# A decode step on one core: all eight sets in PE's loop, wide copies, and the first rows of wo loaded in strided pieces

## The chip, the cores and the metric

The kernel runs on one core of one Trainium2 chip. A core has a matrix engine (PE, whose weight loads are listed as PEld), a vector engine (DVE), a scalar engine (ACT), GpSimd (POOL), a sync engine (SP), and 16 DMA engines that move data between HBM and SBUF. The engines run their own instruction streams and meet at semaphores. DMA requests are issued here from SP and, a few, from ACT; each of the two has its own queue, and within a queue requests are served in order.

The metric is the time of one execution in device microseconds (us), as the median of several runs.

## The reference

One decode step for four batch rows `x` (4 x 512). It computes `g * a + (1 - g) * b`, all inputs bf16:

- `g = sigmoid(sum(x * gate_w))`, one number per row.
- `a`: attention with 32 query heads and 8 KV heads of width 128. `q = x @ wq` (512 x 4096). Each group of four query heads attends to the last 4096 positions of its KV head: scores `q . k / sqrt(128)`, softmax, weighted sum of `v`. The 4096 results per row are multiplied by `wo` (4096 x 512).
- `b`: `h = relu(x @ W_gate) * (x @ W_up)` (both 512 x 1792), then `h @ W_down` (1792 x 512).

There are 4 batch rows x 8 KV heads, so 32 pairs of a 4096 x 128 K block and a V block of the same size, 1 MB each. With the weights some 81 MB are read in all; the output is 4 KB.

## The kernel before, in words

The work is cut into eight **sets** (`NSET`): set s is batch row s // 2 with four KV heads (s % 2 says which half). The K of a set is one DMA of 4 MB into `Ksb[:, s % 2]`, its V one of 4 MB into `Vsb[:, s % 2]`; both are double-buffered. A partition of K holds 128 positions of one head.

Everything is written out by hand. A small class `Program` (line 38) records each engine's operations in order with the named events that each waits for, and emits them as semaphore waits. PE's list has a loop (`Fori`, line 134); all other engines' lists are straight.

Order of requests on SP: wq (line 568, before the block), K0, K1, V0, K2, V1, and so on (lines 231 to 234), then W_gate and W_up into K's buffer 0, V7, W_down into V's buffer 0, and wo in five pieces into `Wbig` (lines 243 to 249). Request K(s) waits until the last scores of set s - 2 are computed (`("SC", s-2, 3)`), V(s) until the last weighted sum of set s - 2 (`("PV", s-2, 3)`). `Wbig` holds wq first; so wo's requests wait for the event `Q`, the last product with wq.

Per set, in PE's order:

- `maximum(s-1)`, `exponent(s-1, k)`, `turn(s-1, k)`: the softmax of the set before. DVE reduces four maxima to a column (L398), PE spreads it over the partitions (L400), DVE takes the minimum (L403), ACT takes the exponential in two pieces of 1024 columns with their sums (L411), DVE transposes each piece in 32 x 32 blocks (L418).
- `kt(s, i)`, 16 **fills** per set: PE transposes four 128 x 128 blocks (two bf16 taken as one fp32) into one of four PSUM banks (L363), and ACT (11 of 16, `ACT_TAKES`) or DVE (the others) copies the bank back over K in SBUF (L368, L370).
- `scores(s, bank)`, four times: eight products of 512 columns on four 32-column strips of the array (L384); then one DVE pass adds the mask and takes the maximum (L392).
- `values(s-1, k)`: four times 16 products with V (L429), then ACT copies the sum (L435).
- `combine(s-2)`: 8 products that gather the heads (L443), the sums of the exponentials (L447), reciprocal and scaling on DVE (L450, L451).

Sets 0 and 1 are written straight on PE; sets 2 to 7 run as three turns of the loop, two sets each. After the loop: the softmax of set 7, `combine(6)`, `gateup` (L459), `values(7)`, `combine(7)`, then `product` (L530): 14 x 4 products with W_down and 32 x 4 with wo, each of 128 columns on one of four column strips, waiting for each piece of wo as it lands. ACT and DVE copy two strips each (L548, L550), and SP sends the output (L574).

## Time and profile before

| What | Value |
|---|---|
| Median of 3 runs | 196.29 us (196.19 to 196.31) |
| Profiled execution: span from first to last instruction | 194.9 us |
| Mean granted PE clock in it | 0.889 |
| Moved by DMA | 81.16 MB, mean 416 GB/s |
| PE, DVE, ACT, POOL busy | 139.4, 77.2, 76.1, 9.5 us |

The profile is of one execution of its own; no time but its span is recorded for it. The runs' median lies 1.4 us above that span, as the span begins with the first and ends with the last instruction on an engine.

How to read the rows that follow. The DMA line of the page cuts the span into 40 slices of 4.87 us; a digit is the mean busy share of the 16 DMA engines in tenths. The queue rows give packets, MB and the time that the packets took as a share of 16 engines' span. A row of the timeline reads: start, length, engine, line, operation, written tile <- read tiles, shapes, number of merged instructions, and in brackets how long the engine idled before and what ended that. A row of a group ends in busy time, mean length of one in ns, and the idle time before. A row of windows reads: stretch, its length, busy time of PE, PEld, DVE, ACT and POOL (number of instructions), the granted PE clock, the DMA share, GB/s. A row of a DMA issue ends in KB and the median us from the issue to the landing.

### The profile page before, as it was taken

Reading aid. Unit: us, or ns where it says so; the run is one execution under the profiler, and the core shown is the slowest. Engines: PE = TensorE matmul, PEld = TensorE weight load, DVE = VectorE, ACT = ScalarE, POOL = GpSimd, SP = SyncE. Lnnn points to the kernel's source line nnn. Section 1 sums busy time; section 2 is a strip of 40 time slices with the busy share of each in tenths; the row PEclk is TensorE's granted clock in tenths of the full one; section 3 lists DMA queues with packets and bytes.
Section 4 is the critical chain, followed back from the end, with each engine's and each line's share of the span. In section 5 each row is a group of like instructions: output and inputs, shape, how many; then the busy total and the mean of one; then the engine's idle time right before and its main releaser. Section 6 shows DMA issues by size and latency. Waiting matters only on the chain.

```text
span 194.9 us, 3931 instructions
## 1 busy us (share of the span) xinstructions
PE 139.4 (72%) x1728; PEld 103.6 (53%) x1728; DVE 77.2 (40%) x169; ACT 76.1 (39%) x140; POOL 9.5 (5%) x41
## 2 busy tenths in 40 slices
PE   0135399688789818996898189995995899643834
PEld 0112397366468517763685177854773777422633
DVE  0100045477268302762583026623952456280101
ACT  2005136494285404462854043445641545240001
POOL 8700000000000000000000000000000000000000
PEclk9999999999999995899999855799999579995855
DMA  6999999999999999999999999999999999998993
GB/s 216 444 437 430 430 444 434 430 430 430 440 430 417 437 427 430 437 437 427 430 430 444 430 437 430 430 430 430 430 430 430 430 386 427 479 430 381 429 397 102
DMA packets 3884, 81.16 MB, mean 416 GB/s; under 512 B 409, under 2 KB 930, under 8 KB 1058
## 3 DMA queue, kind: packets, MB, share of 16 engines
q1 hardware_dynamic: 3864, 81.01, 97.3%
q8 instruction: 8, 0.13, 0.3%
q14 instruction: 2, 0.02, 0.0%
q10 hardware_dynamic: 10, 0.01, 0.0%
HBM read 81.01 MB, written 0.00 MB: 416 GB/s over the span
## 4 chain that ended last, share of the span: by engine, by line
DMA 55%; PE 36%; ACT 4%; DVE 3%; issue 1%; SPq 1%; DVEq 0%
DMA Ksb<-in_A_k_cache_dram 43%; PE bank L363 23%; DMA Wbig<-in_A_wo_dram 11%; PE bank L384 6%; ACT Ksb L368 3%; PE bank L429 2%; PE bank L443 2%; DVE Ksb L370 1%; PE bank L530 1%; ACT L411 1%; ACT sc L411 1%; DVE pT L418 1%; PE bank L447 0%; DVE sc L392 0%; PE bank L400 0%
## 5 line engine op out<-in xcount | busy, mean ns | idle before, releaser
L363 PE MATMUL bank<-identw,Ksb 128*128 128x128 f32 x512 | 77.0, 307 | 20.8 <-DMA Ksb<-in_A_k_cache_dram 14.9
L363 PEld LDWEIGHTS bank<-identw,Ksb 128*128 128x128 f32 x512 | 65.3, 158 | 31.6 <-DMA Ksb<-in_A_k_cache_dram 15.8
L368 ACT COPY Ksb<-bank 128x512 f32<-128x512 f32 x88 | 48.7, 589 | 73.0 <-PE bank L363 73.0
L370 DVE COPY Ksb<-bank 128x512 f32<-128x512 f32 x40 | 27.3, 684 | 40.6 <-PE bank L363 40.6
L392 DVE CUSTOM_DVE_ANT_0 sc<-bank,mask 128x512 bf16<-128x512 f32 x32 | 21.8, 682 | 28.8 <-PE bank L384 28.8
L429 PE MATMUL bank<-Vsb,pT 128*32 128x256 bf16 x512 | 20.9, 291 | 6.1 <-DMA Vsb<-in_A_v_cache_dram 6.1
L384 PE MATMUL bank<-Ksb,qS 128*32 128x512 bf16 x256 | 21.0, 405 | 1.8 <-ACT Ksb L368 0.9
L418 DVE STREAM_TRANSPOSE pT<-sc 128x1024 bf16<-128x1024 bf16 x16 | 19.7, 1236 | 2.1 <-ACT sc L411 2.0
L429 PEld LDWEIGHTS bank<-Vsb,pT 128*32 128x32 bf16 x512 | 13.3, 101 | 12.6 <-issue 8.8
L411 ACT ACTIVATE sc<-sc,negmax 128x1024 bf16<-128x1024 bf16 x16 | 18.4, 1151 | 1.9 <-DVE negmax L403 1.8
L443 PEld LDWEIGHTS bank<-osb,Wsel 128*64 128x64 f32 x128 | 9.4, 157 | 4.8 <-issue 3.7
L443 PE MATMUL bank<-osb,Wsel 128*64 128x32 f32 x128 | 10.3, 239 | 0.5 <-ACT osb L435 0.5
L435 ACT COPY osb<-bank 128x256 f32<-128x256 f32 x8 | 3.0, 373 | 17.6 <-PE bank L429 17.6
L400 PE MATMUL bank<-identw,mcol 128*128 128x128 f32 x16 | 3.8, 320 | 7.8 <-DVE mcol L398 4.7
L384 PEld LDWEIGHTS bank<-Ksb,qS 128*32 128x32 bf16 x256 | 4.1, 95 | 9.0 <-ACT Ksb L368 5.7
L400 PEld LDWEIGHTS bank<-identw,mcol 128*128 128x128 f32 x16 | 2.4, 187 | 10.2 <-DVE mcol L398 8.4
L343 POOL COPY qS<-qW 128x64 bf16<-128x64 bf16 x8 | 1.8, 238 | 120.5 <-PE bank L384 110.8
L530 PE MATMUL bank<-Wbig,oq 128*4 128x128 bf16 x128 | 4.2, 307 | 3.8 <-DMA Wbig<-in_A_wo_dram 3.8
L296 PE MATMUL bank<-identw,xw 5*128 5x5 f32 x4 | 0.6, 263 | 8.6 <-DVE xw L290 8.6
L450 DVE RECIPROCAL recip<-bank 64x1 f32<-64x1 f32 x8 | 1.3, 159 | 11.4 <-PE bank L447 11.4
L530 PEld LDWEIGHTS bank<-Wbig,oq 128*4 128x4 bf16 x128 | 3.1, 118 | 4.8 <-DMA Wbig<-in_A_wo_dram 4.7
L314 PE MATMUL bank<-Wbig,xT 128*32 128x512 bf16 x32 | 3.6, 631 | 2.7 <-DMA Wbig<-in_A_wq_dram 2.7
(55 smaller groups left out, 45.4 us busy)
## 6 DMA issues: line engine op xcount, KB each, us to landing
Ksb<-in_A_k_cache_dram SPq DMA_DIRECT2D x8, 4096.0 KB, 21.8
Vsb<-in_A_v_cache_dram SPq DMA_DIRECT2D x8, 4096.0 KB, 30.9
Wbig<-in_A_wq_dram SPq DMA_DIRECT2D x1, 4096.0 KB, 12.2
Wbig<-in_A_wo_dram SPq DMA_DIRECT2D x1, 2048.0 KB, 19.5
Ksb<-in_B_W_gate_dram SPq DMA_DIRECT2D x1, 1792.0 KB, 17.1
Ksb<-in_B_W_up_dram SPq DMA_DIRECT2D x1, 1792.0 KB, 21.0
Vsb<-in_B_W_down_dram SPq DMA_DIRECT2D x1, 1792.0 KB, 15.0
Wbig<-in_A_wo_dram SPq DMA_DIRECT2D x1, 1280.0 KB, 22.1
```

What stands on the lines that cost most here:

```text
L314: P.op("pe", lambda e, half=half, t=t, g=g, col=col: e.matmul(SCB[half][32 * g:32 * g + 32, 0:512], xT[:, t, :], Wq3[:, t, col:col + 512], ...
L363: P.op("pe", lambda e, bk=bk, cc=cc, c=c, s=s: e.transpose(bk[:, cc * 128:(cc + 1) * 128], Kw[:, s % 2, c * 128:(c + 1) * 128], identw[:, :]),
L368: P.op("act", lambda e: e.copy(dst, bk[:, :]), ("KTC", s, i), [("KT", s, i)], sem="va")
L370: P.op("dve", lambda e: e.tensor_copy(dst, bk[:, :]), ("KTC", s, i), [("KT", s, i)], sem="vd")
L384: P.op("pe", lambda e, a=a, o=o: e.matmul(bk[32 * a:32 * a + 32, 0:512], qS[:, s % 2, o, :], k4[:, 16 * bank:16 * bank + 16, 32 * a:32 * a ...
L392: P.op("dve", lambda e: e.tensor_tensor_reduce(sc[:, s % 2, bank * 512:(bank + 1) * 512], bk[:, :], mask[:, :], 1.0, LOWEST, ALU.add, ALU.max,
L400: P.op("pe", lambda e: e.matmul(TR[NTR - 1][:, 0:128], mcol[:, par:par + 1].to_broadcast([128, 128]), identw[:, :], start=True, stop=True) ...
L411: P.op("act", lambda e: e.activation(sc[:, par, k * PW:(k + 1) * PW], sc[:, par, k * PW:(k + 1) * PW], ACTF.Exp, bias=negmax[:, par:par + ...
L418: P.op("dve", lambda e: e.transpose(pT[:, par, k * PW:(k + 1) * PW], sc[:, par, k * PW:(k + 1) * PW]), ("PTT", s, k), [("EXP", s, k), ("PV ...
L429: P.op("pe", lambda e, c=c, g=g, blk=blk: e.matmul(OB[32 * g:32 * g + 32, 0:256], pT[:, par, 32 * blk:32 * blk + 32], Vsb[:, par, 256 * bl ...
L443: P.op("pe", lambda e, k=k, lo=lo: e.matmul(FB[r, 384:416], Wsel[:, lo:lo + 64], osb[:, par, 32 * k:32 * k + 32], start=(k == 0), stop=(k ...
L530: P.op("pe", lambda e: e.matmul(AB[32 * cb:32 * cb + 4, 0:128], stat, mov[:, 128 * cb:128 * cb + 128], start=start, stop=stop, tile_positi ...
```

## The change

- *PE's loop.* All eight sets run in the loop, as four turns of two. Set -1 is a dummy: its `maximum` and its 64 `values` products run in the first turn on whatever lies there (pT's buffer 1 is zeroed by POOL, mx's too), and its result is not copied.
- *Wide operations.* A fill is eight transposes into two PSUM banks and one copy of 1024 columns; 8 fills per set, two buffers (`NTR`), 5 copies on ACT and 3 on DVE. Scores come in two pairs of banks: 16 products, one DVE pass of 1024 columns; the second pass starts its maximum from the first one's, so the separate reduction is gone. Exponential and DVE transpose take a set's 2048 columns at once. `values` runs its 64 products in one go after the last scores.
- *combine.* It is taken out of the sets. `osb` and `rowsum` keep all sets; after the loop `combine(0)` treats sets 0, 2, 4, 6 and, after the last `values`, `combine(1)` treats sets 1, 3, 5, 7, with 128-column products.
- *wq* is loaded into V's buffer 1 instead of `Wbig`, so V1's request now waits for the dummy `values(-1)`, and wo's requests wait for nothing.
- *wo.* The first three rows of each partition (3,072 bytes) are no longer in SP's pieces. ACT issues them after `gateup`'s ReLU, as twelve transfers: transfer a takes the partitions a, a + 12, a + 24, and so on, 11 in eight of them, 10 in four.
- *Products at the end.* Two strips of 256 columns instead of four of 128; one copy each on DVE and ACT.
- *Borders.* ACT, DVE and PE begin with an instruction that places the following one at a border of 128 (ACT, DVE) or 256 (PE) instructions.

```diff
-NTR = 4
-NSC = 2
-NPIECE = 2
-NBANK = 4
-NFILL = 16
-WO_CUTS = (0, 16, 26, 30)
-ACT_TAKES = (0, 1, 4, 6, 8, 9, 11, 12, 13, 14, 15)
-LOOP_FIRST = 2
-LOOP_TURNS = 3
+NTR = 2
+NPAIR = 2
+NFILL = 8
+WO_EARLY = 3
+WO_CUTS = (3, 16, 26, 30)
+ACT_TAKES = (1, 3, 4, 6, 7)
...
-        Wq3 = Wbig[:, :].rearrange("p (t w) -> p t w", t=4)
+        Wq3 = Vsb[:, 1, :].rearrange("p (t w) -> p t w", t=4)
...
         def load_v(s):
             P.dma("sp", lambda e: e.dma_start(Vsb[:, s % 2, :], heads(A_v_cache, s)), ("V", s),
-                  [("PV", s - 2, 3)] if s >= 2 else [], sem=loop_sem("V", s))
+                  [("PV", s - 2)] if s >= 1 else [], sem=loop_sem("V", s))
...
+        P.op("act", lambda e: e.addr_align(128, offset=0, max_nops=0))
+        P.op("dve", lambda e: e.addr_align(128, offset=0, max_nops=0))
+        P.op("pe", lambda e: e.addr_align(256, offset=0, max_nops=0))
...
-            P.dma("sp", lambda e, lo=lo, hi=hi: e.dma_start(Wbig[:, lo:hi], wo_src[:, lo:hi]), ("WO", k), [("Q",)])
+            P.dma("sp", lambda e, lo=lo, hi=hi: e.dma_start(Wbig[:, lo:hi], wo_src[:, lo:hi]), ("WO", k))
...
+            bk = TRT[:, 1024 * (f % NTR):1024 * (f % NTR) + 1024]
+            for cc in range(8):
+                c = 8 * i + cc
+                w = [("K", s), ("IDENTW",), fills[f - NTR] if f >= NTR else ("QR", 1, f)] if cc == 0 else []
...
+            P.op("dve", lambda e: e.tensor_tensor_reduce(
+                sc[:, s % 2, pair * 1024:(pair + 1) * 1024], SCT[:, :], mask[:, :], 1.0,
+                mx[:, s % 2, 0:1] if pair else LOWEST, ALU.add, ALU.max,
+                mx[:, s % 2, pair:pair + 1]), ("SCC", s, pair), w, sem="vd" if pair else "dve")
...
+            P.op("pe", lambda e: e.matmul(FB[:, 384:512], mx[:, par, 1:2].to_broadcast([128, 128]), identw[:, :],
+                                          start=True, stop=True),
+                 ("MT", s), [("SCC", s, 1)] if s >= 0 else [("XTC",)])
...
+        def values(s):
+            par = s % 2
+            for blk in range(64):
+                g = blk % 4
+                w = [("PTT", s), ("V", s), ("OSB", s - 1)] if blk == 0 else []
+                P.op("pe", lambda e, g=g, blk=blk: e.matmul(
+                    OB[32 * g:32 * g + 32, 0:256], pT[:, par, 32 * blk:32 * blk + 32],
+                    Vsb[:, par, 256 * blk:256 * blk + 256],
+                    start=(blk < 4), stop=(blk >= 60), tile_position=(0, 32 * g)),
+                    ("PV", s) if blk == 63 else None, w)
...
+        def combine(half):
...
+                P.op("pe", lambda e, k=k, lo=lo: e.matmul(CB[r, 0:128], Wsel[:, lo:lo + 64], ov[:, half, :, 32 * k:32 * k + 32],
+                                                          start=(k == 0), stop=(k == 7)), None,
+                     [("OSB", last), ("WSUM",)] + fills[-NTR:])
...
+        for s in range(NSET):
+            if s % 2 == 0:
+                P.turn_edge()
             maximum(s - 1)
+            exponent(s - 1)
+            for i in range(5):
+                kt(s, i)
+                if i == 2:
+                    turn(s - 1)
             scores(s, 0)
+            for i in range(5, NFILL):
+                kt(s, i)
             scores(s, 1)
+            values(s - 1)
         P.turn_edge()
         maximum(NSET - 1)
+        exponent(NSET - 1)
+        turn(NSET - 1)
+        combine(0)
         gateup()
+        early = 0
+        for n, (a, rows) in enumerate([(a, 11) for a in range(8)] + [(a, 10) for a in range(8, 12)]):
+            part = slice(a, a + 12 * (rows - 1) + 1, 12)
+            P.dma("act", lambda e, part=part: e.dma_start(Wbig[part, 0:512 * WO_EARLY], wo_src[part, 0:512 * WO_EARLY]),
+                  ("WOE", n), [], sem="wos")
+            early += 16
+        P.events[("WOE",)] = ("wos", early, None, 0)
+        values(NSET - 1)
+        combine(1)
...
+        def product(stat, mov, u, start, stop, name, waits):
+            P.op("pe", lambda e: e.matmul(AB[32 * u:32 * u + 4, 0:256], stat, mov[:, 256 * u:256 * u + 256],
+                                          start=start, stop=stop, tile_position=(0, 32 * u)), name, waits)
...
+        for i in range(WO_EARLY):
+            for u in range(2):
+                product(oq3[:, :, i], Wo3[:, i, :], u, False, False, None, [("WOE",), ("OQ", 0), ("OQ", 1)])
...
+        P.op("dve", lambda e: e.tensor_copy(outr[:, 0:256], AB[0:4, 0:256]), ("FIN", 0), [("ACC", 0)], sem="fin")
+        P.op("act", lambda e: e.copy(outr[:, 256:512], AB[32:36, 0:256]), ("FIN", 1), [("ACC", 1)], sem="fin")
...
-        nc.sync.dma_start(Wbig[:, :], A_wq.rearrange("(p t) w -> p (t w)", p=128)).then_inc(sems["wq"], 16)
+        nc.sync.dma_start(Vsb[:, 1, :], A_wq.rearrange("(p t) w -> p (t w)", p=128)).then_inc(sems["V1"], 16)
```

More of the change, by code (lines that the diff above doesn't have):

```diff
@@ L307, in bass_gated_mix__sliding_block_cached__glu_gated_reglu__decode_kernel @@
         P.op("act", lambda e: e.activation(gsb[:, 4:8], FB[:, 32:36], ACTF.Sigmoid, scale=-1.0), ("G",), sem="va")
-        for half in range(2):
-            for t in range(4):
+        for t in range(4):
+            for half in range(2):
                 for g in range(4):
@@ L389, in scores @@
-            w = [("SC", s, bank), ("MASK",)]
-            if s >= 2 and bank == 0:
-                w += [("PTT", s - 2, NPIECE - 1), ("MCOL", s - 2)]
+                for hb in range(2):
+                    for a in range(4):
+                        w = []
+                        if first:
+                            w = [("KTC", s, 4 * pair + u) for u in range(4)] + [("QS", s)]
+                            w.append(("SCC", s, 0) if pair else ("SCC", s - 1, 1) if s >= 1 else ("QR", 1, 1))
+                        first = False
+                        bank = 2 * pair + hb
+                        P.op("pe", lambda e, a=a, o=o, hb=hb, bank=bank: e.matmul(
+                            SCT[32 * a:32 * a + 32, 512 * hb:512 * hb + 512], qS[:, s % 2, o, :],
+                            k4[:, 16 * bank:16 * bank + 16, 32 * a:32 * a + 32, o], start=(o == 0), stop=(o == 1),
+                            tile_position=(0, 32 * a)),
+                            ("SC", s, pair) if (a == 3 and o == 1 and hb == 1) else None, w)
@@ L516, in bass_gated_mix__sliding_block_cached__glu_gated_reglu__decode_kernel @@
         P.turn_edge()
         maximum(NSET - 1)
-        for k in range(NPIECE):
-            exponent(NSET - 1, k)
-            turn(NSET - 1, k)
-        combine(NSET - 2)
+        exponent(NSET - 1)
+        turn(NSET - 1)
+        combine(0)
         gateup()
-        for k in range(4):
-            values(NSET - 1, k)
-        combine(NSET - 1)
-        AB = SCB[0]
+        early = 0
[4 more added lines that the diff above has]
+            early += 16
```

258 lines of the change are left out of this document (95 added, 163 removed).

## The prediction

> **What bounds the kernel now.** I read the page first: the span, the engines' shares, the DMA slices and the queues (packets, MB, share of 16 engines).
>
> ```profile
> span 194.9 us, 3931 instructions
> PE 139.4 (72%) x1728; PEld 103.6 (53%) x1728; DVE 77.2 (40%) x169; ACT 76.1 (39%) x140; POOL 9.5 (5%) x41
> DMA  6999999999999999999999999999999999998993
> q1 hardware_dynamic: 3864, 81.01, 97.3%
> q8 instruction: 8, 0.13, 0.3%
> q14 instruction: 2, 0.02, 0.0%
> q10 hardware_dynamic: 10, 0.01, 0.0%
> ```
>
> The 16 DMA engines are busy 97.3% of the span, while PE idles over a quarter of it. Moving 81 MB is the bound; what can be won lies where the DMA slices are not 9: the first slice (same requests, same order, after the change too) and the last few. So I cut the end into half microseconds (columns: length, then busy time of PE, PEld, DVE, ACT, POOL, then PE clock, DMA share, GB/s), and then read the timeline there (start, length, engine, line).
>
> ```profile
> 190.00:190.50 0.50, 0.00 (x0) 0.00 (x0) 0.00 (x0) 0.00 (x0) 0.00 (x0) 0.50 0.92 316
> 190.50:191.00 0.50, 0.09 (x8) 0.10 (x12) 0.00 (x0) 0.00 (x0) 0.00 (x0) 0.50 0.63 246
> 191.00:191.50 0.50, 0.50 (x24) 0.50 (x24) 0.00 (x0) 0.00 (x0) 0.00 (x0) 0.50 0.57 200
> 191.50:192.00 0.50, 0.50 (x26) 0.36 (x16) 0.00 (x0) 0.00 (x0) 0.00 (x0) 0.50 0.56 166
> 192.00:192.50 0.50, 0.50 (x24) 0.34 (x18) 0.00 (x0) 0.00 (x0) 0.00 (x0) 0.50 0.28 71
> ```
>
> ```profile
> 172.37 0.52 ACT L464 ACTIVATE hrelu<-bank 128x448 f32<-128x448 f32 x1
> 178.67 3.61 PE L429 MATMUL bank<-Vsb,pT 128*32 128x256 bf16 x64 [6.06 <-DMA Vsb<-in_A_v_cache_dram]
> 182.74 1.12 PE L443 MATMUL bank<-osb,Wsel 128*64 128x32 f32 x16 [0.47 <-ACT osb L435]
> 184.00 1.20 PE L530 MATMUL bank<-Vsb,hT 128*4 128x128 bf16 x56
> 187.77 1.88 PE L530 MATMUL bank<-Wbig,oq 128*4 128x128 bf16 x64 [2.57 <-DMA Wbig<-in_A_wo_dram]
> 190.91 2.30 PE L530 MATMUL bank<-Wbig,oq 128*4 128x128 bf16 x64 [1.25 <-DMA Wbig<-in_A_wo_dram]
> 192.82 0.10 PEld L530 LDWEIGHTS bank<-Wbig,oq 128*4 128x4 bf16 x4 [0.17 <-DMA Wbig<-in_A_wo_dram]
> 192.98 0.54 ACT L550 CAST outr<-bank 4x128 bf16<-4x128 f32 x2 [10.29 <-PE bank L530]
> 192.98 0.60 DVE L548 CAST outr<-bank 4x128 bf16<-4x128 f32 x2 [8.35 <-PE bank L530]
> 193.61 0.35 SPq L574 DMA_DIRECT2D out_dram<-outr  x1
> ```
>
> From 190.5 to 192.0 the share stands near 0.56, which is 9 engines of 16: seven have finished, nine run on. Every load gives each engine the same bytes, so something delayed nine. The page names it: ten instruction packets. The eight of q8 take 0.3% of 16 x 194.9, 9.4 us or 1.17 us each, and each sits on one engine. In half microseconds, 0.63 + 0.57 + 0.56 + 0.28 is 1.02 us of all engines; spread evenly it would end at 191.5 and not 192.5. PE waits for the last piece of wo until 192.82, so this unevenness is on the path, and so are the last copies.
>
> **The change part by part.**
>
> *Strided first rows of wo.* Three of the 32 rows of wo in each partition (128 pieces of 3,072 bytes) leave the SP queue for twelve ACT transfers of 11 or 10 rows. The queue q10 above carried a four-row and a one-row transfer in ten packets: five rows and five completions, so a short transfer uses as many engines as rows. If each begins at the same engine, ten engines take 12 rows, one takes 8 and five take none. 430 GB/s over 16 is 26.9 GB/s per engine: an even share is 24.6 KB or 0.91 us; 12 rows are 1.37 us. So five engines end 0.91 us earlier, ten 0.46 us later. If the five are the delayed ones, they end at 192.5 - 0.91 = 191.6, the others near 190.9 + 0.46 = 191.4: the last landing moves by -0.91. If they aren't, it moves by up to +0.46. I take -0.91: it is nearest to the 1.02 that an even end gives.
>
> [...]
>
> Twelve issues stand on ACT between the ReLU (172.37 + 0.52) and the last copy to osb, which needs the products that end at 182.28.
>
> ```profile
> 0.80 0.56 ACTq L229 DMA_DIRECT2D xsb<-in_A_x_dram  x1
> 1.40 0.23 ACTq L230 DMA_DIRECT2D xsb<-in_gate_w_dram  x1
> ```
>
> At 0.23 to 0.56 each they end at 175.7 to 179.6: covered; without cover up to 6.7 us. Without [Q], SP's wo requests only queue behind Wd's, as before.
>
> *All sets in PE's loop; borders.* Counted over the two programs, 956 PE products as written become 585, so the eight q8 packets should become about five, and the two of q14 go if ACT's and DVE's shorter programs fit their block. Five packets of 1.17 us over 16 engines are 0.4 us; zero if the remaining ones meet badly. I take -0.1. The jump to a border may cost PE, ACT or DVE a fetch at the start, but PE's first product waits until 8.57 for x, and set 0 until 22.72 for K. A loop fetched anew each turn would show in the middle; it doesn't, with two back edges inside:
>
> ```profile
> 8.57 0.64 PE L296 MATMUL bank<-identw,xw 5*128 5x5 f32 x4 [8.57 <-DVE xw L290]
> ```
>
> ```profile
> q1 hardware_dynamic: 1514, 37.83, 100.0%
> ```
>
> The second is the only queue row of 92 to 180 us.
>
> *Wide operations, and where they could let the DMA run dry.* These set when K and V buffers come free. Prices: twice the 512-wide rows, as upper bounds. The rows are groups (busy, mean ns), the timeline, and DMA issues (KB, us to landing: K2's alone, all K, wq).
>
> ```profile
> L368 ACT COPY Ksb<-bank 128x512 f32<-128x512 f32 x88 | 48.7, 589 | 73.0 <-PE bank L363 73.0
> L370 DVE COPY Ksb<-bank 128x512 f32<-128x512 f32 x40 | 27.3, 684 | 40.6 <-PE bank L363 40.6
> L392 DVE CUSTOM_DVE_ANT_0 sc<-bank,mask 128x512 bf16<-128x512 f32 x32 | 21.8, 682 | 28.8 <-PE bank L384 28.8
> ```
>
> ```profile
> 22.72 6.57 PE L363 MATMUL bank<-identw,Ksb 128*128 128x128 f32 x32 [4.50 <-DMA Ksb<-in_A_k_cache_dram]
> 29.77 1.97 PE L363 MATMUL bank<-identw,Ksb 128*128 128x128 f32 x16
> 163.75 0.62 PE L429 MATMUL bank<-Vsb,pT 128*32 128x256 bf16 x16
> ```
>
> ```profile
> Ksb<-in_A_k_cache_dram SPq DMA_DIRECT2D x1, 4096.0 KB, 17.5
> Ksb<-in_A_k_cache_dram SPq DMA_DIRECT2D x8, 4096.0 KB, 21.8
> Wbig<-in_A_wq_dram SPq DMA_DIRECT2D x1, 4096.0 KB, 12.2
> ```
>
> Eight transposes take 0.98 at full clock (1.97/2), a copy 1.2 to 1.4. With two buffers I follow the order: fills 0 to 4 end 5.8 us after K landed, first scores 7.0 (16 products, twice 0.62), fill 7 waits for DVE's copy behind its transpose and its masked pass and ends at 11.0, last scores 13.5, values 16.0 (four times 0.62). A set lasts 19.4 us by DMA. A K request lands after 21.8 us, its own 4.19 MB taking 9.7 and the start 12.2 - 9.7 = 2.5; so 9.6 us of delay are covered. Set 0 is tightest: K2's request (the 17.5 row, issued 35.68) has 5.3 us of cover, so until 41.0. Starting cold at 0.205 per transpose, I get the last score at 37.6. Covered by 3.4. The 64 dummy values of set 0 (2.5 us) delay V1's request to 40.1, behind the 9.7 us of K2; the two pool memsets and the wider mask end long before 35 us. The wait of each of these is PE's, and behind it stand only its own set's products. Cost nothing; uncovered, each us late is a us. Nothing here can gain, since the queue row above has the engines at 100.0%.
>
> *The end.* combine for all sets of a half comes after the last values: 16 products of 128 columns, 1.97 (as the transposes) and not 1.12. A product row now is two products of 256 columns on two column strips, not four of 128 on four: 256-column groups cost (0.62 - 0.27)/3 = 0.117 at full clock (0.27 being one product's length at the end of sixteen) and 3.61/16 = 0.226 at half. At full: 182.74 + 1.97 + 0.4 + 14 x 0.117 + 3 x 0.117 = 187.1, when wo's 13 rows have landed (187.77 - 0.91 = 186.9); they end at 188.6, the next ten (190.0) at 191.2, four at 191.7, and the last two, landing at 191.9, 0.39 later, against 0.16 before: +0.23. One 256-wide copy, 0.37 as the osb copy,
>
> ```profile
> L435 ACT COPY osb<-bank 128x256 f32<-128x256 f32 x8 | 3.0, 373 | 17.6 <-PE bank L429 17.6
> ```
>
> takes the place of two (0.60): -0.23.
>
> *Sum* against the profiled span: 194.93 - 0.91 - 0.10 + 0.23 - 0.23 = 193.92. The runs' median, 196.29, lies 1.36 above that span; I keep this: **195.3 us**.
>
> **The rivals.**
>
> *Half clock at the end (slower).* The clock rows, in its own windows:
>
> ```profile
> 117.40:120.80 3.40, 3.40 (x29) 2.23 (x27) 2.19 (x4) 1.65 (x3) 0.00 (x0) 0.50 1.03 443
> 178.80:182.20 3.40, 3.40 (x64) 2.57 (x57) 0.00 (x0) 0.00 (x0) 0.00 (x0) 0.50 1.01 429
> 182.20:185.60 3.40, 2.50 (x80) 2.04 (x76) 0.49 (x2) 0.37 (x1) 0.00 (x0) 1.00 0.98 411
> 185.60:189.10 3.50, 1.33 (x52) 1.33 (x56) 0.00 (x0) 0.00 (x0) 0.00 (x0) 0.51 0.98 410
> ```
>
> Before, the last products run at 0.50, which four strips can afford. With two strips at 0.226 the 13 rows end at 189.8, ten at 192.3, four at 193.2, the last four products near 194.0: 1.7 later than my 192.3, so **197.0**; half clock from the combine on would cost about 4. It decides if the clock is half when the ten rows land. For it: 185.6 on. Against: the longer streams are more work per window (1.5 us of wo's 13 rows beside 2.0 of Wd and the early rows, where a combine and 1.20 of short products lost it).
>
> [...] The trace agrees at 178.80 but not at 117.40, fully busy at 0.50 and followed by 0.50; so I leave this rival 17%.
>
> *Relief on the wrong engines (no change).* If fetches fall on the ten loaded engines, these end at 192.5 + 0.46, less what fewer fetches give (0.4): **196.3**. For: no row says which engines fetch. Against: nine were late before, so fewer must be now.
>
> *Set 0 late.* Cold clock through set 0: fills 8 x 1.7, scores 2 x 1.9, copies: the last score near 41.5, half a us dry: **195.8**; more if DVE's wide passes stall PE.
>
> **How the numbers follow.** Forecast 0.61, own range 194.5 to 195.7 (-1.02 and -0.4 in full below; half of the relief above); half clock 0.17; wrong engines 0.13; set 0 or a fetch stall 0.09 (half of it over 196.7). A measurement tells 0.2%, 0.4 us, from no change: faster 0.65 (the forecast and half of set 0), same 0.11 (wrong engines but for 0.02), slower 0.24 (half clock and the rest). The range, 194.5 to 197.0, reaches from the forecast's lower bound to half clock's price and leaves out the dearer half of that case and the worst stalls, under 0.2.
>
> **What would show it.** Right: q8 at five packets or fewer, q14 at none after the start; DMA share over 0.85 until it drops within half a us; the last wo landing near 191.9; middle windows at share 1.00. Wrong: share near 0.5 for over a us at the end (wrong engines), PE never waiting for wo at clock 0.50 (half clock), a slice under 9 near 41 us (set 0).

## The result, and the profile after

The changed kernel takes **199.45 us** (median, 199.33 to 199.51) against 196.25 for the kernel before on the same chip (196.19 to 196.31): a ratio of **1.0163** [1.0151, 1.0176]. It is slower by 3.2 us, where 195.3 was forecast and 194.5 to 197.0 given as the range. In the experiments, one execution each of three versions (without borders, twelve on SP's queue, four neighbouring) lay over 1.5% above that version's fastest and is left out of the times given below, so the four neighbouring stand at 198.34 where a later expectation has 198.46.

The page of the changed kernel (span; DMA share in 40 slices; queues with packets, MB, share of 16 engines):

```profile
span 198.2 us, 3511 instructions
...
PE 130.7 (66%) x1578; PEld 102.7 (52%) x1578; DVE 73.8 (37%) x95; ACT 66.4 (34%) x77; POOL 11.6 (6%) x43
...
DMA  6999999999999999999999999999999999999980
...
q1 hardware_dynamic: 3864, 80.61, 96.1%
q10 hardware_dynamic: 266, 0.40, 0.6%
q8 instruction: 5, 0.08, 0.2%
q14 instruction: 2, 0.02, 0.0%
```

The span grew from 194.9 to 198.2. No slice ran dry, and the engines do less work than before (PE 130.7 against 139.4). The same 81 MB took longer. Where, the windows show (length; busy time of PE, PEld, DVE, ACT, POOL; PE clock, DMA share, GB/s), first of the changed kernel, then of the kernel before:

```profile
60.00:170.00 110.00, 80.63 (x964) 65.01 (x963) 50.39 (x59) 43.40 (x47) 0.95 (x4) 0.91 1.00 430
...
176.50:181.00 4.50, 1.63 (x32) 1.42 (x36) 0.00 (x0) 0.00 (x0) 0.00 (x0) 0.56 0.98 372
181.00:187.00 6.00, 5.53 (x85) 4.52 (x75) 0.64 (x3) 0.37 (x1) 0.00 (x0) 0.76 1.00 363
187.00:191.50 4.50, 0.27 (x6) 0.00 (x0) 0.00 (x0) 0.00 (x0) 0.00 (x0) 0.91 0.99 355
191.50:195.00 3.50, 3.50 (x42) 2.37 (x44) 0.00 (x0) 0.00 (x0) 0.00 (x0) 0.63 0.46 166
```

```profile
176.50:181.00 4.50, 2.33 (x48) 2.03 (x51) 0.00 (x0) 0.00 (x0) 0.00 (x0) 0.50 0.97 412
181.00:187.00 6.00, 3.70 (x100) 2.73 (x92) 0.49 (x2) 0.37 (x1) 0.00 (x0) 0.78 1.00 419
187.00:191.50 4.50, 2.48 (x88) 2.19 (x92) 0.00 (x0) 0.00 (x0) 0.00 (x0) 0.50 0.88 347
191.50:195.00 3.50, 1.71 (x50) 0.95 (x40) 0.56 (x2) 0.52 (x2) 0.00 (x0) 0.50 0.12 35
```

From 176.5 on the engines are as busy as before (share 0.98 to 1.00) but move 372 and 363 GB/s in place of 412 and 419. A full share at a lower rate means that each packet takes longer (the records below: 0.61 us in place of 0.54). The timeline of the changed kernel (start, length, engine, line; in brackets the idle time before and what ended it) says what is in flight then:

```profile
24.56 6.47 PE L356 MATMUL TRT<-identw,Ksb 128*128 128x128 f32 x32 [3.37 <-DMA Ksb<-in_A_k_cache_dram]
...
39.10 0.53 SPq L218 DMA_DIRECT2D Ksb<-in_A_k_cache_dram  x1
...
172.43 9.39 ACTq L504 DMA_DIRECT2D Wbig<-in_A_wo_dram  x12
...
179.37 3.60 PE L425 MATMUL OB<-Vsb,pT 128*32 128x256 bf16 x64 [6.81 <-DMA Vsb<-in_A_v_cache_dram]
...
183.02 0.37 ACT L434 COPY osb<-OB 128x256 f32<-128x256 f32 x1 [10.06 <-PE OB L425]
...
191.50 4.91 PE L514 MATMUL SCT<-Wbig,oq 128*4 128x256 bf16 x64 [4.23 <-DMA Wbig<-in_A_wo_dram]
196.44 0.41 DVE L531 CAST outr<-SCT 4x256 bf16<-4x256 f32 x1 [10.05 <-PE SCT L514]
196.48 0.36 ACT L532 CAST outr<-SCT 4x256 bf16<-4x256 f32 x1 [13.09 <-PE SCT L514]
196.88 0.35 SPq L553 DMA_DIRECT2D out_dram<-outr  x1
```

The twelve strided transfers of wo are issued from 172.43 to 181.82. In the trace's packet records their rows run from 176.7 to 190.5, and exactly there a packet of SP's loads takes 1.15 times its usual length (median; 14,336 bytes: 0.61 us in place of 0.54). Only 5 of the 379 load packets in that stretch are within 3% of their usual length. The records do not name the engine. But in the kernel before, the first three loads of 4 MB start their packets of 32,768 bytes in 24 rounds of 16, eight rounds to a load (from 1.84 to 31.5 us), so the same bytes for every engine; if wo's pieces are dealt out alike, none of the 16 can have been spared. Before and after that stretch the factor is 1.00.

So the 3.3 us of span divide. The last packet of wo ends at 194.55 and not 192.37: **+2.2**. PE stands idle for the early rows until 191.50 and then has all 64 products of wo ahead of it, 4.91 us long, much of it at half clock (0.50 until 194.0); its last work ends at 196.44 and not 192.98, which is **+1.3** more than the landing. The copies to the output request take 0.44 in place of 0.63: **-0.2**.

### The profile page after: what moved, and what is told of

Same layout as the page of the kernel before. It is cut to its first block, busy times and chain, and to the rows that moved or that the text cites. A ratio compares the mean times of both kernels' runs of the same rounds, so it can differ in the third digit from the quotient of the medians.

```text
span 198.2 us, 3511 instructions
## 1 busy us (share of the span) xinstructions
PE 130.7 (66%) x1578; PEld 102.7 (52%) x1578; DVE 73.8 (37%) x95; ACT 66.4 (34%) x77; POOL 11.6 (6%) x43
## 4 chain that ended last, share of the span: by engine, by line
DMA 53%; PE 23%; DVE 13%; ACTq 4%; ACT 3%; issue 2%; PEld 1%; PEldq 0%; SPq 0%
DMA Ksb<-in_A_k_cache_dram 47%; PE TRT L356 14%; DVE Ksb L363 6%; DMA Wbig<-in_A_wo_dram 5%; ACTq L504 4%; DVE pT L417 3%; PE SCT L377 3%; ACT Ksb L361 3%; DVE sc L387 3%; PE SCT L514 3%; PE TRT L444 1%; PE OB L425 1%; PE TRT L461 1%; PEld OB L425 1%; PEldq L133 0%
## 5 line engine op out<-in xcount | busy, mean ns | idle before, releaser
L356 PE MATMUL TRT<-identw,Ksb 128*128 128x128 f32 x512 | 75.8, 309 | 24.2 <-DMA Ksb<-in_A_k_cache_dram 16.2
L356 PEld LDWEIGHTS TRT<-identw,Ksb 128*128 128x128 f32 x512 | 66.8, 160 | 34.4 <-DMA Ksb<-in_A_k_cache_dram 17.4
L361 ACT COPY Ksb<-TRT 128x1024 f32<-128x1024 f32 x40 | 40.5, 1012 | 57.9 <-PE TRT L356 57.8
L363 DVE COPY Ksb<-TRT 128x1024 f32<-128x1024 f32 x24 | 29.3, 1223 | 39.6 <-PE TRT L356 39.6
L425 PE MATMUL OB<-Vsb,pT 128*32 128x256 bf16 x576 | 18.9, 288 | 6.8 <-DMA Vsb<-in_A_v_cache_dram 6.8
L377 PE MATMUL SCT<-Ksb,qS 128*32 128x512 bf16 x256 | 16.9, 381 | 8.8 <-ACT Ksb L361 8.8
L425 PEld LDWEIGHTS OB<-Vsb,pT 128*32 128x32 bf16 x576 | 16.4, 101 | 9.7 <-issue 7.2
L387 DVE CUSTOM_DVE_ANT_0 sc<-SCT,mask,mx 128x1024 bf16<-128x1024 f32 x8 | 10.3, 1285 | 26.8 <-PE SCT L377 26.8
L407 ACT ACTIVATE sc<-sc,negmax 128x2048 bf16<-128x2048 bf16 x8 | 16.0, 2002 | 11.0 <-DVE negmax L399 11.0
L417 DVE STREAM_TRANSPOSE pT<-sc 128x2048 bf16<-128x2048 bf16 x8 | 18.4, 2302 | 2.2 <-ACT sc L407 2.2
```

The lines of the kernel that those rows point to most:

```text
L356: P.op("pe", lambda e, bk=bk, cc=cc, c=c: e.transpose(bk[:, cc * 128:(cc + 1) * 128], Kw[:, s % 2, c * 128:(c + 1) * 128], identw[:, :]), ...
L361: P.op("act", lambda e: e.copy(dst, bk), ("KTC", s, i), [("KT", s, i)], sem="va")
L363: P.op("dve", lambda e: e.tensor_copy(dst, bk), ("KTC", s, i), [("KT", s, i)], sem="vd")
L377: P.op("pe", lambda e, a=a, o=o, hb=hb, bank=bank: e.matmul(SCT[32 * a:32 * a + 32, 512 * hb:512 * hb + 512], qS[:, s % 2, o, :], k4[:, 16 ...
L387: P.op("dve", lambda e: e.tensor_tensor_reduce(sc[:, s % 2, pair * 1024:(pair + 1) * 1024], SCT[:, :], mask[:, :], 1.0, mx[:, s % 2, 0:1] ...
L407: P.op("act", lambda e: e.activation(sc[:, par, :], sc[:, par, :], ACTF.Exp, bias=negmax[:, par:par + 1], scale=SCALE, accum_out=rowsum[:, ...
```

## The experiments

The first question was whether the early rows are the loss at all; my theory after the result was that they are, through the slow packets. The rival was the change's other parts: the loop, the wide operations, the fetches at the start.

### Without the early rows

The twelve transfers go, `WO_CUTS` is `(0, 16, 26, 30)` again; loop, borders, wide operations and two strips stay.

```diff
-WO_CUTS = (3, 16, 26, 30)
+WO_CUTS = (0, 16, 26, 30)
-        early = 0
...
-        P.events[("WOE",)] = ("wos", early, None, 0)
```

> The changed kernel with wo's first three rows back in SP's first piece, nothing else undone. Theory 1 (the twelve early transfers cost it): DMA rate stays near 430 GB/s from 176 to 190 us, the last piece of wo lands near 192.8 and not 195.0, PE does not wait for early rows, time 195.8 to 196.6. Rival (the loop, the wide operations or the fetches at the start cost it, and the early transfers are only there beside it): time above 198.0, and the last landing stays late.

196.26 us (195.87 to 198.4), ratio 0.9999 [0.999, 1.0009]. In the median, the early rows are the whole loss. The landing did not come out as expected: the profiled execution is the longest of the eleven, 198.4, and its last packet of wo ends at 194.53, not near 192.8, although its packets keep their usual length (factor 1.00 from 176.7 to 190.5). The reason stands behind the table of packet records below.

### The borders, and borders and early rows together

```diff
-        P.op("act", lambda e: e.addr_align(128, offset=0, max_nops=0))
-        P.op("dve", lambda e: e.addr_align(128, offset=0, max_nops=0))
-        P.op("pe", lambda e: e.addr_align(256, offset=0, max_nops=0))
```

> The changed kernel without the three border alignments; the strided transfers stay. Theory 1 (the early transfers are the loss, and a code fetch costs one DMA engine 1 to 2 us wherever it falls, so moving the fetches to the start only moves that price): K0 lands about 1.8 us earlier, near 22.7, but fetches come back in the middle; 198.8 to 199.6. Rival (the start fetches are a price of their own that the missing middle ones do not give back): 197.4 to 198.4.

> The changed kernel with neither the early rows nor the three alignments: the loop over all sets, the wide operations, the shorter end and the two strips are left. Theory 1: within 0.3 of the kernel before, 195.9 to 196.5. Rival (the start fetches hide a gain of the loop and the wide operations): 194.4 to 195.4, and this version would beat both kernels.

Without the borders but with the early rows: median 198.91 us, but from 197.63 to 199.41, ratio 1.01 [1.007, 1.013]. The median lies where theory 1 put it; the scatter is too wide to weigh tenths. K0's first transpose is at 22.8 us again and not at 24.56: the 1.84 us of the start are the borders' price. With neither, 196.16 us, ratio 0.9994 [0.9985, 1.0003], beside 196.26 with the borders: in the median, the price at the start does not reach the end. In the median, the loop, the wide operations and the end of the changed kernel gain nothing and lose nothing that can be measured.

### One transfer, eight, twelve neighbouring

Why are the packets slow? One ACT transfer of 128 partitions; eight strided ones of 16 partitions, one row for every engine by their completions (q10 has 266 packets: the ten of before, 128 rows, and 128 completions, so 16 to a transfer); twelve of neighbouring partitions in place of strided ones.

```diff
-        for n, (a, rows) in enumerate([(a, 11) for a in range(8)] + [(a, 10) for a in range(8, 12)]):
-            part = slice(a, a + 12 * (rows - 1) + 1, 12)
# one
+        for n, part in enumerate([slice(0, 128)]):
# eight, stride 8
+        for n, a in enumerate(range(8)):
+            part = slice(a, a + 8 * 15 + 1, 8)
# twelve neighbouring
+        for n, (a, rows) in enumerate([(11 * a, 11) for a in range(8)] + [(88 + 10 * a, 10) for a in range(4)]):
+            part = slice(a, a + rows)
```

> The early rows as one ACT transfer of all 128 partitions in place of twelve. [...] If two active queues as such slow the packets: 14336-byte packets near 0.6 us for as long as it is in flight, and time above 198. If it is the assignment of partitions to engines (or the strided order in HBM) in the twelve: rate stays near 430 GB/s, time 195.8 to 196.8.

> [...] If it is the strided order in HBM, or two active queues, or many small transfers: rate near 360 GB/s while they are in flight, time above 198.

> The early rows as twelve ACT transfers of 11 or 10 neighbouring partitions: as many as before, the same engines by number of rows, but not strided. If it is the strided order in HBM: rate near 430 GB/s, time 196 to 197. If it is the assignment of partitions to engines, or two active queues: rate near 360 GB/s and time near 199.

One: 196.77 us, ratio 1.0048 [1.0017, 1.0079], packets at 1.01 times their length. Eight: 198.22, 1.01 [1.0083, 1.0117], packets at 1.24. Twelve neighbouring: 200.22, 1.0201 [1.0178, 1.0223], packets at 1.20. So a second queue as such does not slow the loads, and slow packets need neither a stride (the twelve neighbouring, at 200.22 even above the 199 expected) nor engines that get no rows (the eight). The assignment of partitions to engines seemed to be out too, because the eight were meant to keep the one of the large loads. But no row shows which engine writes which partition, so the price of the eight says nothing against the assignment, and the partitions come back below. At this point, what the dear ones had in common seemed to be that they are many and small.

### Many and small?

The twelve transfers put on SP's queue ahead of wo's first piece; four strided ACT transfers of 32 partitions; eight of 32 partitions and half the columns; four of 16 partitions and one of 64; five of 22 and one of 18.

```diff
# twelve on SP
+            P.dma("sp", lambda e, part=part: e.dma_start(Wbig[part, 0:512 * WO_EARLY], wo_src[part, 0:512 * WO_EARLY]),
# four, stride 4
+            part = slice(a, a + 4 * 31 + 1, 4)
# eight, stride 4, half the columns
+            part, cols = slice(n // 2, n // 2 + 4 * 31 + 1, 4), slice(768 * (n % 2), 768 * (n % 2) + 768)
# four of 16 and one of 64
+        for n, part in enumerate([slice(16 * a, 16 * a + 16) for a in range(4)] + [slice(64, 128)]):
# five of 22 and one of 18
+        for n, part in enumerate([slice(22 * a, min(22 * a + 22, 128)) for a in range(6)]):
```

> The same twelve strided transfers, put on SP's queue ahead of wo's first piece, so that they are alone in one queue with the loads and nothing is on ACT's queue. Theory 1a (many small transfers cost by themselves, in whatever queue): 197.0 to 199.0, with early rows' packets still slow. Theory 1b (they cost only beside a second queue's load, because each engine goes back and forth between two queues): 195.3 to 196.5, packets of 14336 B back at 0.54.

> The early rows in four ACT transfers of 32 partitions at stride 4, between the one transfer (196.77) and the eight (198.22). Theory 1 (the price grows with the number of transfers): 197.2 to 197.9, 14336 B packets at 0.56 to 0.62 while they are in flight. Rival (only transfers of 16 rows or fewer are dear): 196.3 to 196.9, packets at 0.54.

> Eight ACT transfers like the dear eight (198.22), but each of 32 partitions and half the columns (1536 B a row), so that every engine gets two rows of each transfer instead of one; the number of transfers and of their completions is the same. Theory 2 (what is dear is a transfer that gives an engine one single row): 196.1 to 196.8, 14336 B packets at 0.54. Rival (what is dear is the number of transfers and completions): 197.6 to 198.8, packets at 0.60 or more while they are in flight.

> Four ACT transfers of 16 partitions (one row an engine) for partitions 0 to 63, and one transfer for 64 to 127. Theory 2: half of the 64-of-128 single rows, so half of the loss of the eight: 196.9 to 197.6. Rival (five transfers are too few to hurt, as four were): 196.1 to 196.6.

> The early rows in five ACT transfers of 22 partitions and one of 18, two rows an engine, so that some engines are relieved of them as in the twelve, but without single rows. Theory 2: no slow packets; what is left is the relief: 195.3 to 196.4. Rival (leaving engines out is itself dear): 197.0 to 199.0.

On SP's queue: 199.81 us (198.82 to 200.02), above the 199.0 that theory 1a allowed. Here the early rows are alone in one queue with the loads, and while they run (180.3 to 185.5 in the packet records) the rate falls furthest:

```profile
176.50:180.50 4.00, 1.61 (x32) 1.41 (x36) 0.00 (x0) 0.00 (x0) 0.00 (x0) 0.50 0.95 402
180.50:185.50 5.00, 4.53 (x76) 3.85 (x69) 0.64 (x3) 0.37 (x1) 0.00 (x0) 0.88 1.06 263
185.50:190.00 4.50, 1.27 (x22) 0.58 (x16) 0.00 (x0) 0.00 (x0) 0.00 (x0) 1.00 0.96 389
```

Theory 1b, two queues, falls with that. Four at stride 4: 196.36, 1.0006 [0.9997, 1.0016], no slow packets. Eight at stride 4 with half the columns: packets at 1.01, which takes the number of transfers off the list. Its time, 198.14 (196.48 to 199.3; 1.0087 [1.0052, 1.0122]), is not explained by that: it missed theory 2's time while it bore out its packets. Its rows come in 256 smaller packets and land only at 189.6. Its last packet of wo ends at 193.94, 1.4 us later than with four transfers. In the profiled execution (198.89) about as much was lost long before the early rows, near 42 us, as shown behind the table of packet records.

Theory 2, single rows, fell with the other two: five transfers of 22 rows and one of 18, by my estimate two rows for each engine that takes part (four transfers of 32 rows had 202 - 10 - 128 = 64 completions, so 16 each), gave 199.04, 1.0147 [1.013, 1.0164], packets at 1.24. Four of 16 and one of 64 gave 198.93, 1.013 [1.0113, 1.0147], at 1.29, more than the rival's "too few to hurt" and more than the half that theory 2 allowed.

### Before the early rows are waited for

The products of the early rows moved behind those of wo's three pieces.

> The changed kernel, with the products of the early rows moved behind those of wo's three pieces: PE no longer stands still for the early rows. If the loss is PE's wait for them (4.23 us): 196.5 to 197.5. If it is the loads, of which the last lands 2.2 us later: the last landing stays near 195.0, the end moves by at most 1.2 us: 198.0 to 199.0.

The profiled execution took 198.47 us with a span of 197.2, 1.0 less than the changed kernel's, the last packet of wo at 194.53 as there. That fits: PE's wait is worth about 1, the loads the rest. But the median is 200.16 (198.47 to 201.01; 1.0217 [1.0191, 1.0242]), above both expected ranges, so the 1.3 of the split above is read from the trace and not confirmed by the runs.

### The place, the spread, and the change's other parts

The twelve transfers alone in the kernel before; four of 32 neighbouring partitions; two of 88 and 40 neighbouring ones; the twelve at the very start of ACT's program.

```diff
# four, neighbouring
+        for n, part in enumerate([slice(32 * a, 32 * a + 32) for a in range(4)]):
# 88 and 40
+        for n, part in enumerate([slice(0, 88), slice(88, 128)]):
```

> The kernel before with one part of the change alone: the twelve strided transfers on ACT's queue and the first three blocks of wo's products waiting for them. If the early rows are the whole loss, whatever loop and operations stand around them: 198.6 to 200.0, with 14336 B packets at 0.58 or more while they are in flight. If they only hurt together with the change's loop and wide operations: 195.5 to 196.6.

> Four ACT transfers of 32 neighbouring partitions instead of 32 at stride 4 (196.36). Theory 3 (what is dear is a transfer of fewer than 32 rows, wherever the rows lie): 196.1 to 196.8, packets at 0.54. Rival (what is dear is that the rows read at one time are neighbours, as in the contiguous twelve, the six and the half): 197.8 to 199.2, packets at 0.60 or more.

> Two ACT transfers, of 88 and of 40 neighbouring partitions, which leave engines out as the twelve do (88 rows as eight on each of eleven engines), but in large transfers. Theory 3 (few rows in a transfer are dear, not the uneven spread): packets at 0.54, 195.4 to 196.6. Rival (a spread over some of the engines alone is dear): packets at 0.60 or more, 197.8 to 199.5.

> The twelve strided transfers issued at the very start of ACT's program, beside the loads of wq and of the first K, instead of near the end. If the slow packets come with these transfers wherever they stand: K0 lands 2 to 4 us later than in the changed kernel and the end is 198.0 to 200.0. If they belong to the mix of loads at the end: 195.3 to 196.8, and this would be the way to have the early rows.

In the kernel before, the twelve alone cost 2.2 of the change's 3.2 us: 198.38 us, just under the 198.6 to 200.0 expected, 1.0134 [1.0092, 1.0176], packets at 1.15. At the start they slow K's packets instead, to 1.07 over 29 us. K0's first transpose comes at 26.00 and not 24.56, 1.4 us later where 2 to 4 were expected, and the end is late again: 198.59, 1.0126 [1.0108, 1.0144]. The 88 and 40: 198.93, 1.0153 [1.0092, 1.0213], at 1.28, so large transfers can be dear too. And four neighbouring: 198.34, 1.0112 [1.0092, 1.0132], at 1.24, where the same four at stride 4 cost nothing. Theory 3, few rows, is out as well. What is left is *which rows go where*.

### Which side of the transfer

Stride 4 in SBUF's partitions alone, and in the rows of wo alone.

```diff
+            part, rows = slice(a, a + 4 * 31 + 1, 4), slice(32 * a, 32 * a + 32)
# into partitions at stride 4, out of neighbouring rows
+            P.dma("act", lambda e, part=part, rows=rows: e.dma_start(Wbig[part, 0:512 * WO_EARLY], wo_src[rows, 0:512 * WO_EARLY]),
# into neighbouring partitions, out of rows at stride 4
+            P.dma("act", lambda e, part=part, rows=rows: e.dma_start(Wbig[rows, 0:512 * WO_EARLY], wo_src[part, 0:512 * WO_EARLY]),
```

> Four ACT transfers of 32 rows: into partitions at stride 4, as in the one that cost nothing (196.36), but out of neighbouring rows of wo, as in the one that cost 2 us (198.46). It puts wo's first three blocks in the wrong partitions, so these products are not the reference's. If what counts is which partitions an engine writes: packets at 0.54, 196.0 to 196.8. If what counts is which rows of wo are read at one time: packets at 0.60 or more, 198.0 to 199.2.

> The other way round: into 32 neighbouring partitions, out of rows of wo at stride 4 (again the wrong rows for the products). If what counts is which partitions an engine writes: packets at 0.60 or more, 198.0 to 199.2. If what counts is which rows of wo are read at one time: packets at 0.54, 196.0 to 196.8.

Into partitions at stride 4: 196.36 us, 1.0007 [0.9997, 1.0016]. Into neighbouring partitions: 198.37, 1.0105 [1.0088, 1.0121]. The windows of the two, the cheap one first:

```profile
176.50:181.00 4.50, 1.73 (x36) 1.53 (x40) 0.00 (x0) 0.00 (x0) 0.00 (x0) 0.50 0.99 415
181.00:184.00 3.00, 2.53 (x39) 1.88 (x32) 0.00 (x0) 0.37 (x1) 0.00 (x0) 0.50 1.01 426
...
187.00:191.50 4.50, 2.80 (x50) 1.88 (x46) 0.00 (x0) 0.00 (x0) 0.00 (x0) 1.00 0.89 350
191.50:195.00 3.50, 1.95 (x28) 1.00 (x24) 0.41 (x1) 0.36 (x1) 0.00 (x0) 1.00 0.08 24
```

```profile
176.50:181.00 4.50, 1.02 (x20) 0.89 (x24) 0.00 (x0) 0.00 (x0) 0.00 (x0) 0.50 0.95 314
181.00:184.00 3.00, 2.58 (x51) 1.79 (x40) 0.00 (x0) 0.37 (x1) 0.00 (x0) 0.50 1.04 345
...
187.00:191.50 4.50, 3.22 (x56) 2.19 (x52) 0.39 (x2) 0.00 (x0) 0.00 (x0) 1.00 0.96 403
191.50:195.00 3.50, 2.09 (x32) 1.36 (x32) 0.00 (x0) 0.00 (x0) 0.00 (x0) 1.00 0.51 176
```

With the same number of rows, transfers, engines and bytes (202 packets in q10 in each), and rows of wo read the other way round, the share is full in both, and the rate is 415 and 426 in one, 314 and 345 in the other, until the early rows are through. With the two four-transfer versions before them (196.36 with both sides at stride 4, 198.34 with both neighbouring), all four combinations are measured: the partitions decide, not the rows of wo.

The packet records of the runs with early rows, side by side (median length of a load's packet while early rows are in flight, as a multiple of its usual length; end of wo's last packet, us):

```
                                    factor  in flight        wo ends
one transfer of 128                  1.01   175.1 to 181.7   192.97
four of 32, partitions at stride 4   1.01   176.1 to 183.4   192.52
  the same, rows neighbouring        1.01   175.1 to 183.0   192.60
eight of 32, stride 4, half width    1.01   176.1 to 189.6   193.94
twelve strided (the change)          1.15   176.7 to 190.5   194.55
  in the kernel before               1.15   176.1 to 190.5   194.59
  without borders                    1.12   175.3 to 190.1   194.36
  early rows waited for last         1.15   176.1 to 190.2   194.53
  at the start                       1.07     6.0 to  35.0   194.46
  on SP's queue                      1.70   180.3 to 185.5   194.91
twelve neighbouring                  1.20   175.0 to 190.4   195.22
eight of 16, stride 8                1.24   175.3 to 186.6   194.84
five of 22 and one of 18             1.24   174.7 to 187.9   195.13
four of 16 and one of 64             1.29   176.8 to 187.8   196.91
four of 32, neighbouring             1.24   174.9 to 184.8   194.50
  rows at stride 4                   1.26   174.7 to 184.6   194.39
88 and 40                            1.28   175.5 to 186.0   195.12
```

The factor is the firmer of the two columns, as the end is that of one execution. Broadly, the factor is milder the longer the rows are in flight: 1.70 at 5.2 us, 1.24 to 1.29 at 9.9 to 13.2, 1.12 to 1.15 at 13.8 to 14.8, 1.07 at 29.0; the twelve neighbouring, 1.20 at 15.4, stand out. An estimate of the loading time lost is the time in flight times (1 - 1/factor): 1.8 us for 13.8 us at 1.15, 1.9 for 29.0 at 1.07, 1.9 for 9.9 at 1.24, 2.1 for 5.2 at 1.70, 2.6 for 15.4 at 1.20. The dear ones all lose 1.6 to 2.6 us of loading for the same 128 rows, whenever and in whatever portions, and their times lie 2 to 4 us up.

Three profiled executions hold a second loss, which has nothing to do with the early rows. The rows below give, in pairs, the request of K2 and the ten microseconds around its start: for the changed kernel (39.10, shown above, so its windows alone), without early rows, eight of 32 at half width, and four of 16 with one of 64.

```profile
38.00:48.00 10.00, 9.33 (x140) 7.08 (x141) 6.28 (x8) 6.34 (x7) 0.24 (x1) 1.00 1.02 433
```

```profile
39.15 0.54 SPq L217 DMA_DIRECT2D Ksb<-in_A_k_cache_dram  x1
38.00:48.00 10.00, 9.27 (x139) 7.06 (x140) 6.22 (x7) 6.38 (x8) 0.24 (x1) 1.00 0.92 377
```

```profile
39.32 0.54 SPq L218 DMA_DIRECT2D Ksb<-in_A_k_cache_dram  x1
38.00:48.00 10.00, 9.14 (x138) 7.02 (x138) 6.05 (x7) 6.34 (x8) 0.24 (x1) 1.00 0.91 357
```

```profile
39.36 0.54 SPq L218 DMA_DIRECT2D Ksb<-in_A_k_cache_dram  x1
38.00:48.00 10.00, 9.07 (x138) 6.92 (x138) 6.01 (x7) 6.38 (x8) 0.24 (x1) 1.00 0.93 351
```

Where K2 was requested at 39.10 or earlier, as in 16 of the 20 profiled executions, the engines had work throughout (all 16 together lost under 0.1 us). Requested at 39.15 to 39.36, it came too late: between 41.1 and 44.0 us, as few as 9, 6 and 7 engines had a packet in flight, and the ten microseconds moved 377, 357 and 351 GB/s in place of 433. Against 430 GB/s this is 1.2, 1.7 and 1.8 us of loading lost. (With the twelve at the start, K2's request at 39.61 did no harm, because the loads ahead of it were some 3 us late themselves: K0's first transpose at 26.00, where the kernel before has 22.72.) So the late ends of these three (194.53, 193.94 and 196.91) are not to be put down to the early rows alone: the first has none, the second has no slow packets, the third lost time both ways. Whether other long executions, of which there is no trace, had the same cause is not shown.

## Why the prediction was wrong

**Strided first rows of wo: here it failed.** The step said that moving 12 rows to an engine adds 1.37 us to that engine and to no other, and took -0.91 for the last landing, with +0.46 as the worst end. The landing moved by +2.2 (192.37 to 194.55). The mistake is the row of 26.9 GB/s per engine taken as a price that holds wherever an engine writes. The runs show that the same 128 rows cost nothing (196.36 us) or 2 us (198.37), by the SBUF partitions that one transfer takes together, and that the price falls on nearly all packets of the loads (374 of 379 more than 3% longer), not only on the engines that carry the extra rows.

*Why the partitions decide* no run shows, and none was made to test a cause. The loads' packets stayed at 1.01 times their length with all 128 partitions in one transfer and with 32 at stride 4. They grew to between 1.07 and 1.70 times with 10 or 11 at stride 12, to 1.20 with 10 or 11 neighbouring ones, to 1.24 with 16 at stride 8 and with 22 and 18, and to between 1.24 and 1.29 with 32 neighbouring ones, with 16 and 64, and with 88 and 40. The number of engines does not part them: the four transfers at stride 4 and the four neighbouring have the same 202 packets in q10, 64 of them completions. The size is open too: at the prediction's 26.9 GB/s per engine, 128 rows are 0.91 us of all engines, and the loading lost, by the estimate above, was 1.6 to 2.6.

**The relief.** How many engines a transfer uses was right, by the completions: q10's 266 packets are the ten of before, 128 rows and 128 completions. The two large transfers (88 and 40) have 159 - 10 - 128 = 21, which fits the eleven engines expected for the 88 rows and leaves ten for the 40:

```profile
q10 hardware_dynamic: 159, 0.40, 0.6%
```

Which engines took the rows no row shows. That the five without rows are the delayed ones, as the -0.91 has it, was my estimate; the last landing moved by +2.2.

The reading of the uneven end before, engines delayed by instruction packets, fits one more trace. Of the ten packets, one starts only at 192.39, which leaves nine for the nine late engines. The version without early rows and borders has six such packets before 191, and its share from 191.5 to 192 is 0.38 in place of 0.56, six engines of 16:

```profile
191.50:192.00 0.50, 0.50 (x12) 0.19 (x8) 0.00 (x0) 0.00 (x0) 0.00 (x0) 1.00 0.38 112
```

But with the early rows the even end did not come. The half microseconds of the changed kernel:

```profile
191.50:192.00 0.50, 0.50 (x6) 0.34 (x8) 0.00 (x0) 0.00 (x0) 0.00 (x0) 0.50 0.82 320
...
192.50:193.00 0.50, 0.50 (x10) 0.31 (x6) 0.00 (x0) 0.00 (x0) 0.00 (x0) 0.50 0.74 259
193.00:193.50 0.50, 0.50 (x8) 0.34 (x6) 0.00 (x0) 0.00 (x0) 0.00 (x0) 0.50 0.44 153
193.50:194.00 0.50, 0.50 (x8) 0.28 (x6) 0.00 (x0) 0.00 (x0) 0.00 (x0) 0.50 0.31 95
```

From 0.82 it runs down over 2.5 us, where the forecast wanted a fall within half a us. The rival "relief on the wrong engines" saw this, but at 196.3 it held only the uneven end and not the slow packets, the larger part.

**The twelve issues** took 9.39 us, 0.78 each, above the 0.56 that I had as the upper end; they ended at 181.82, still ahead of the copy at 183.02, so the cover held. What I had not costed is that they also spread the landing: the early rows came at 190.5, after the 13 rows that they were to precede, and PE did nothing for 4.23 us.

**Loop and borders: right in sum, wrong in the cover.** q8 fell from eight packets to five, as counted. In the packet records, q14's two moved to the start (4.05 and 6.14 us), so that there were none after it, as forecast; without borders they stand at 94.65 and 105.67. A fetch at the start was called harmless because PE waits for K until 22.72. It did delay K0, by 1.84 us, and K2 was requested at 39.10 (forecast 37.6, plus this delay). That is not well inside a cover until 41.0, as I had it, but at its very edge: the engines ran dry in the executions with K2's request at 39.15 and later. The median did not move (196.26 with borders, 196.16 without), but with borders and no early rows one execution took 198.4, and without borders none took more than 196.52. In the changed kernel the share stood at 1.00 and the rate at 430 GB/s from 60 to 170.

**Wide operations: right in the median.** They cost nothing and won nothing: without borders K2 was requested at 37.26, against 37.6 forecast. In the changed kernel's profiled execution set 0 was not late enough to matter. The rival "set 0 late" did happen, together with the borders, in the three executions named above.

**The end.** Loop, wide operations and end together were forecast at -0.10 + 0.23 - 0.23 = -0.1; the version without early rows and borders stands at 0.9994 [0.9985, 1.0003] of 196.29, -0.1 as well, within what can't be told from zero. The copies measured 0.41 and 0.36 against 0.37 forecast.

**Half clock at the end** was the rival on the right side, but the trace has another course: the rival has the clock at 0.5 when wo lands because the streams are thin. In the changed kernel PE stood idle for the early rows (0.27 us of products in the 4.50 before 191.5), and the clock was 0.50 from 191.0 to 194.0. In the first of the two runs at stride 4 on one side, where PE is busy for 2.80 of the 4.50 us before 191.5, the last windows above show 1.00, as the forecast assumed. What sets the clock no run was made to show: in the kernel before, a stretch fully busy at 0.50 was followed by 1.00 (from 182.20) in one place and by 0.50 (from 120.80) in another, so the 17% was my estimate.

No version beat the kernel before: the fastest, without early rows and borders, equals it.

## What to carry to other kernels

With the DMA engines as the bound, a side transfer wasn't priced by its bytes alone: the partitions that it takes together decided (196.36 against 198.37 us). All 128 partitions in one transfer, or 32 at stride 4, kept the loads' packets at their length here (1.01, against 1.07 to 1.70 in the other patterns); why is not shown. Full share at a lower GB/s in the windows (1.00 and 363 GB/s) was the sign of slow packets; a share below 1 in the middle (0.92 and 377) was the other case, engines without a request. And look at the whole span before a late landing is explained: three traces here held a loss near 42 us that had nothing to do with the rows moved near 180 us. And a load split off to land early is early only if its issues (here 0.78 us each) and its turn on the engines let it (here until 190.5).

## What the runs showed of the hardware that I had not expected

- 0.39 MB in 128 rows, moved beside full loads, cost nothing or 2 us by the partitions alone (196.36 against 198.37 and 198.34 us). In the dear patterns the median packet of the loads grew by 7 to 70% while the rows were in flight, most where they ran in the loads' own queue.
- The request for K2's 4 MB had to be issued about 2 us before the queue ahead of it ran out: K2 requested at 39.10 us left no gap, at 39.15 to 39.36 engines stood without packets from 41.1 us on.
- A jump to a border at the start brought one 16 KB fetch at 2.6 us that took 1.63 us on one engine, and K0 came 1.84 us later, yet the median of this DMA-bound kernel did not move (196.26 against 196.16 us).
